# First layer of chunks 3 to 9 as seven block products in place of eight, in a fused attention and feed-forward kernel

## The chip, the cores and the metric

One Trainium2 chip, one core of it. The metric is device time of one launch in microseconds (us), the median of several runs. A core has TensorE (PE, matmuls into PSUM; its weight loads are the row PEld), VectorE (DVE), ScalarE (ACT), GpSimd (POOL) and SyncE (SP), whose queue issues nearly all DMAs here. PSUM has 8 banks, each 128 partitions by 512 f32.

## What is computed

The reference, cut to what matters (8 batches, 8 heads, 576 positions, head size 64, model width 512, hidden width 2048):

```python
k_p = k.reshape(B, H, Sp, 8, D).mean(axis=3)        # 576 keys pooled to 72; v likewise
attn = softmax(q @ k_p.T / sqrt(D)) @ v_p
x = attn.transpose(0, 2, 1, 3).reshape(B, S, 512)
xn = (x - mean(x)) / sqrt(var(x) + 1e-6) * g_ln
out = x + relu(xn @ w_ch1) @ w_ch2                  # 512 -> 2048 -> 512
```

The 4608 rows of x are 36 tiles of 128 tokens, or 9 chunks of 512 tokens (4 tiles each). The code counts chunks from 0, so "chunks 3 to 9" are c = 2 to 8.

## The kernel before, in words

**Arithmetic.** TensorE works in f16 here. Every f32 operand of the two layers is held as a pair of f16 parts, high and low, and a product is three matmuls: high by high, high by low, low by high. The weights come as 8-byte floats; `load_raw` fetches a block of 1 MB, `convert` makes f32 of it, `split_w` scales it and splits it into the pair in `wt`.

**Attention, per tile t.** `stage_a(t)` loads q two tiles ahead, `scores(t)` makes the scores (8 PE instructions, L284), DVE takes the maximum and subtracts it (L293, L294), `probs(t)` runs exp on ACT (L303), casts to f16 (L304), forms the low part on POOL (L311) and transposes the pair by a DMA on SP's queue (L321). `values(t)` multiplies by V (16 instructions, L340 and L341, into PSUM tile `ps_x`; more where a tile lies in two batches), divides by the sums (DVE L354, ACT L361), computes mean and variance and an inverse root (DVE L365 to L383), normalises to `z` (L387), casts to the high part (ACT L391), forms the low part (POOL L392), and transposes the pair into `zT` of its chunk by a DMA (L396).

**Feed-forward, per chunk c.** `ffn_in(c, f)` makes one block of 128 hidden units for all 512 tokens: 4 blocks of the model width times 3 products, 12 matmuls of 512 columns (L415) into one bank of `ps_f`. ACT writes the relu's high part into a ring buffer (L423), DVE its low part (L424). A ring buffer holds a quarter, 4 such blocks. `ffn_out(c, tt, half)` takes the 8 blocks of one half of the hidden width for one tile of tokens: 24 matmuls of 512 columns (L444), and DVE adds the result to x (L454). The second half's result goes out by DMA (L458).

**The order of the work.** Chunks 0 and 1, with the loading, converting and splitting of the weights, follow a list of tokens, `START`: R, C, M and S are the weights' steps, A and B the two attention stages of a tile, HK and HV the pooling of a batch's K and V on POOL, I a quarter of `ffn_in`, O a half of `ffn_out`. From chunk 2 on a loop runs, per chunk, 24 units: 8 `ffn_in`, 4 `ffn_out`, 8 `ffn_in`, 4 `ffn_out`. Before unit number `A_AT[i]` comes the first attention stage of tile i of the next chunk, before `B_AT[i]` the second. A scheduler then orders the instructions of each engine, so that a piece can move some way from where the code has it; each engine works through its order strictly in turn.

**Buffers.** PSUM: 2 banks for scores (`ps_s`), 2 for values (`ps_x`), 4 for the layers (`ps_f`). SBUF: 4 ring buffers, 3 buffers `vr` for loads of V, 2 of `zT`, and 2 buffers of raw weights.

Of the kernel before, what the change touches and what calls it, by code (L numbers as in the profile page):

```python
# [61 lines left out]
def attn_ffn_kernel(ctx: ExitStack, tc: tile.TileContext, qT, kT, v, g, w1, w2, out):  # L62
# [260 lines left out]
    def values(t):  # L323
# [67 lines left out]
        nc.scalar.copy(out=zhl[:, 0, :], in_=z)  # L391
        nc.gpsimd.tensor_tensor(out=zhl[:, 1, :], in0=z, in1=zhl[:, 0, :], op=ALU.subtract)  # L392
# [3 lines left out]
        nc.sync.dma_start_transpose(  # L396
            out=zTs[c][:, :, tt * P : (tt + 1) * P], in_=zhl.rearrange("p a d -> p (a d)")
        )
# [34 lines left out]

# [141 lines left out]
```

## Time and profile before

| | |
|---|---|
| time, median of 3 runs | 895.31 us (894.42 to 897.43) |
| the profiled execution: time, span | 897.94 us, 896.2 us |
| mean granted PE clock | 0.995 of full |
| PE busy | 826.6 us, 92% of the span |
| DVE, ACT, POOL busy | 421.4, 278.8, 259.6 us |
| matmuls of the first layer (L415) | 1824, of them 192 with 256 columns, the rest with 512 |
| matmuls of the second layer (L444) | 1728, all with 512 columns |

The profile is of one execution, whose own time stands beside its span; the 1.7 us between them are outside the instructions. Matmuls overlap in the pipeline, so the time of one alone (some 380 ns for 512 columns) is not what it costs in a row; that is read from the starts of a group.

### The profile page before, as it was taken

What the parts mean: (1) busy time and instruction counts of PE and PEld (TensorE: products, weight loads), DVE (VectorE), ACT (ScalarE), POOL (GpSimd) and SP (SyncE); (2) the same over time, 40 slices, a digit from 0 to 9 for tenths busy, and PEclk for the clock granted to TensorE, in tenths of its full rate; (3) what the DMA queues carried; (4) which work ended last, traced back from release to release, by engine and by line L of the source; (5) the groups of instructions that cost most, each with busy time, mean ns of one, the idle gap of its engine ahead of it and who ended that gap; (6) DMA issues with size and microseconds to landing.
All of it is one profiled execution on the core that took longest, in us unless ns stands there. A gap on an engine that the chain in (4) does not pass through costs nothing.

```text
span 896.2 us, 11921 instructions
## 1 busy us (share of the span) xinstructions
PE 826.6 (92%) x4524; PEld 417.1 (47%) x4524; DVE 421.4 (47%) x970; ACT 278.8 (31%) x529; POOL 259.6 (29%) x414
## 2 busy tenths in 40 slices
PE   2236997999999999999999999999999999999998
PEld 1225744444444444544454545444544454444443
DVE  6587884425643543364335433543354335432121
ACT  2887873313212221233123312331233123311020
POOL 5587783207241340165003610220021002100000
PEclk9999998999999999999999999999999999999999
DMA  8989993102451241254123432341223121310001
GB/s 301 296 219 288 278 269 71 27 4 94 107 128 37 65 101 37 59 145 109 44 53 86 118 65 60 86 89 44 54 59 80 41 54 37 70 47 12 1 1 47
DMA packets 137289, 84.81 MB, mean 95 GB/s; under 512 B 116112, under 2 KB 117264, under 8 KB 135184
## 3 DMA queue, kind: packets, MB, share of 16 engines
q1 hardware_dynamic: 135696, 82.86, 35.2%
q10 hardware_dynamic: 1536, 1.20, 0.5%
q8 instruction: 35, 0.57, 0.3%
q14 instruction: 22, 0.18, 0.1%
HBM read 45.09 MB, written 9.44 MB: 61 GB/s over the span
## 4 chain that ended last, share of the span: by engine, by line
PE 82%; DMA 8%; POOL 6%; issue 2%; ACT 1%; DVE 1%; SPq 1%; POOLq 0%
PE ps_f L444 39%; PE ps_f L415 38%; PE ps_s L284 3%; DMA vr<-in_v_dram 3%; DMA ring<-in_w_dram 1%; POOL vr L234 1%; DMA raw<-in_w_dram 1%; DMA zT<-hl 1%; PE ps_x L340 1%; PE ps_x L341 1%; POOL kr L220 1%; DMA kr<-in_kT_dram 1%; DMA raw<-in_v_dram 1%; POOL kblk L224 1%; POOL kr L221 1%
## 5 line engine op out<-in xcount | busy, mean ns | idle before, releaser
L415 PE MATMUL ps_f<-zT,w 128*128 128x512 f16 (+1 forms) x1824 | 386.3, 371 | 4.4 <-DMA zT<-hl 3.4
L444 PE MATMUL ps_f<-w,ring 128*128 128x512 f16 x1728 | 379.6, 379 | 2.2 <-DVE ring L424 1.2
L415 PEld LDWEIGHTS <-w 128*128 128x128 f16 x1824 | 178.3, 99 | 194.4 <-DMA zT<-hl 3.7
L444 PEld LDWEIGHTS <-ring 128*128 128x128 f16 x1728 | 167.9, 98 | 202.5 <-issue 3.7
L423 ACT ACTIVATE ring<-ps_f 128x512 f16<-128x512 f32 (+1 forms) x152 | 86.6, 573 | 271.0 <-PE ps_f L415 252.4
L424 DVE SCALAR_TENSOR_TENSOR ring<-ps_f,ring 128x512 f16<-128x512 f32 (+1 forms) x152 | 99.7, 660 | 140.5 <-ACT ring L423 138.7
L454 DVE SCALAR_TENSOR_TENSOR x<-ps_f,c_out,x 128x512 f32<-128x512 f32 x72 | 53.8, 749 | 186.8 <-PE ps_f L444 186.8
L311 POOL TENSOR_TENSOR phl<-e,phl 128x512 f16<-128x512 f32 x36 | 42.8, 1190 | 263.9 <-ACT phl L304 262.8
L284 PE MATMUL ps_s<-kblk,q 128*128 128x144 f32 (+1 forms) x320 | 54.6, 333 | 52.8 <-issue 21.8
L392 POOL TENSOR_TENSOR hl<-z,hl 128x512 f16<-128x512 f32 x36 | 42.5, 1181 | 122.4 <-ACT hl L391 120.5
L284 PEld LDWEIGHTS ps_s<-kblk,q 128*128 128x128 f32 (+1 forms) x320 | 47.0, 211 | 60.8 <-issue 39.0
L303 ACT ACTIVATE e<-e 128x576 f32<-128x576 f32 x36 | 24.5, 682 | 155.4 <-DVE e L294 150.8
L361 ACT ACTIVATE x<-ps_x,rs 128x64 f32<-128x64 f32 x144 | 33.3, 312 | 73.5 <-DVE x L354 33.6
L234 POOL TENSOR_TENSOR vr<-vr 72x256 f32<-72x256 f32 x56 | 44.8, 805 | 29.7 <-DMA vr<-in_v_dram 29.2
L224 POOL TENSOR_TENSOR kblk<-kr 64x72 f32<-64x72 f32 x58 | 22.0, 379 | 76.2 <-PE ps_s L284 73.5
L391 ACT CAST hl<-z 128x512 f16<-128x512 f32 x36 | 22.2, 617 | 57.6 <-DVE z L387 57.5
L304 ACT CAST phl<-e 128x1024 f16<-128x1024 f32 x36 | 37.5, 1042 | 6.1 <-issue 3.1
L365 DVE BATCH_NORM_STATS2 st<-x 128x6 f32<-128x512 f32 x36 | 24.9, 692 | 23.4 <-ACT x L361 23.2
L340 PE MATMUL ps_x<-va,pt 128*128 128x65 f16 (+1 forms) x320 | 27.5, 200 | 5.9 <-ACT x L361 4.0
L293 DVE TENSOR_REDUCE mx<-ps_s 128x8 f32<-128x576 f32 x36 | 26.8, 745 | 12.4 <-PE ps_s L284 12.2
L387 DVE TENSOR_SCALAR z<-x,mv,y 128x512 f32<-128x512 f32 x36 | 30.4, 845 | 3.3 <-POOL hl L392 0.8
L380 DVE TENSOR_SCALAR a<-y,ve 128x1 f32<-128x1 f32 x108 | 29.3, 271 | 3.0
(80 smaller groups left out, 470.8 us busy)
## 6 DMA issues: line engine op xcount, KB each, us to landing
raw<-in_w_dram SPq DMA_DIRECT2D x12, 1024.0 KB
q<-in_qT_dram SPq DMA_DIRECT2D x36, 256.0 KB
out_dram<-x SPq DMA_DIRECT2D x36, 256.0 KB
kr<-in_kT_dram SPq DMA_DIRECT2D x30, 288.0 KB
vr<-in_v_dram SPq DMA_DIRECT2D x56, 144.0 KB
ring<-in_w_dram SPq DMA_DIRECT2D x4, 1024.0 KB
raw<-in_v_dram SPq DMA_DIRECT2D x8, 144.0 KB
va<-vh ACTq DMA_DIRECT2D x16, 65.0 KB
```

The costliest lines, as they stand in the source:

```text
L234: eng.tensor_add(out=vr[:, 0:4, :], in0=vr[:, 0:4, :], in1=vr[:, 4:8, :])
L284: nc.tensor.matmul(ps[r, p // 2, p % 2 * 2 * KV : (p % 2 + 1) * 2 * KV], lhsT=q[:, p, r], rhs=kblk[b % NKB][:, p, :], start=True, stop=True,)
L304: nc.scalar.copy(out=ph[:, :, :, 0:KA], in_=e[:, :, 0:KA].unsqueeze(1).broadcast_to([P, 2, H, KA]))
L311: nc.gpsimd.tensor_tensor(out=ph[:, 0, :, KA:P], in0=e[:, :, 0:KA], in1=ph[:, 0, :, 0:KA], op=ALU.subtract)
L340: nc.tensor.matmul(o, lhsT=pt[:, h, r], rhs=VA[b][:, h, :], start=True, stop=False)
L361: nc.scalar.activation(out=xh[:, 4 + i, :], in_=px[:, 1, i, 0:D], func=AF.Copy, scale=rs[:, 4 + i : 5 + i])
L392: nc.gpsimd.tensor_tensor(out=zhl[:, 1, :], in0=z, in1=zhl[:, 0, :], op=ALU.subtract)
L415: nc.tensor.matmul(ps, lhsT=w[:, part, fs], rhs=zT[:, kz, cols], start=(n == 0), stop=(n == 3 * NKT - 1),)
L423: nc.scalar.activation(out=h[:, 0, i, cols], in_=ps, func=AF.Relu)
L424: nc.vector.scalar_tensor_tensor(out=h[:, 1, i, cols], in0=ps, scalar=0.0, in1=h[:, 0, i, cols], op0=ALU.max, op1=ALU.subtract,)
L444: nc.tensor.matmul(ps, lhsT=h[:, part, i, cols], rhs=w[:, wp, j], start=(n == 0), stop=(n == 3 * NFT // 2 - 1),)
L454: nc.vector.scalar_tensor_tensor(out=x, in0=ps, scalar=c_out[:, half : half + 1], in1=x, op0=ALU.mult, op1=ALU.add)
```

## The change

From chunk 2 on, the product of the first layer is done on a 2 by 2 split: the 512 tokens in two halves, the 512 model columns in two halves, the 1024 hidden units of a half of the width in two halves of 512. In place of eight block products there are seven, between sums of blocks (a form of Strassen's method; the table `FACTOR` names the two factors of each). Each product is 2 blocks of the model width times 3, that is 6 matmuls with 256 columns (one half of the tokens).

- **Weights.** `sums_w` forms three sums T2, T3, T4 of the blocks of w1, `sum_last` the fourth, T1, in the place of a block that chunks 0 and 1 no longer need. These are the tokens T and U in `START`, four each.
- **Tokens.** For a tile of the first two of a chunk nothing changes but the place of the transposed pair. For a tile of the last two, `values` normalises the tile two before it once more (`za`), forms the four sums S1 to S4 on DVE, and casts, subtracts and transposes ten blocks (S3, A22, S1, S2, S4) in two pieces of 640 columns in place of one of 512. They go into `zB`, of which there is one; so the transposes of the third tile are held in `pending` and issued at unit 12, behind the last product of the chunk in work.
- **Products.** `ffn_seven(c, h, f)` replaces `ffn_in` for a pair of hidden blocks. Three PSUM banks serve a pair: one takes products 1, 6 and 7 one on top of the other, one 5 and 3, one 2 and then 4. In between ACT copies the partial results to SBUF (four copies of 256 columns per pair), DVE adds to them (four of 256 columns), and relu and low part then run from SBUF (two each of 512 columns).
- **Loop.** 16 units per chunk: 4 `ffn_seven`, 4 `ffn_out`, and again; `A_AT` and `B_AT` are (0, 5, 7, 10) and (4, 6, 11, 12). `ffn_out` takes the two hidden blocks of a pair one after the other, in the order in which the pairs come.
- **Buffers.** 2 ring buffers in place of 4, 2 `vr` in place of 3. Behind `START`, scores and values share one PSUM tile of 2 banks and the layers have 6 banks.
- **START.** O.0.1 goes ahead of I.1.2; R.1.0 and R.1.1 load into the new buffers `tsp`; T and U are put in.

```diff
-A_AT, B_AT = (0, 6, 10, 14), (5, 9, 13, 19)
+A_AT, B_AT = (0, 5, 7, 10), (4, 6, 11, 12)
+FACTOR = {1: ("A11", "B11"), 2: ("A12", "B21"), 3: ("S4", "B22"), 4: ("A22", "T4"), 5: ("S1", "T1"),
+          6: ("S2", "T2"), 7: ("S3", "T3")}
...
-A.10 B.9 I.0.3 S.2.5 S.2.6 HK.3.0 HK.3.1 I.1.2 B.10 S.2.7 O.0.1 I.1.3 A.11 HV.3.0 B.11 HV.3.1 O.1.1
+S.2.5 I.0.3 S.2.6 S.2.7 O.0.1 B.8 T.0.0 HK.3.0 A.10 B.9 T.0.1 HK.3.1 I.1.2 T.1.0 U.0.0 U.0.1 T.1.1 I.1.3
+U.1.0 U.1.1 A.11 HV.3.0 B.10 HV.3.1 B.11 O.1.1
...
-    ring = ctx.enter_context(tc.tile_pool(name="ring", bufs=4))
+    ring = ctx.enter_context(tc.tile_pool(name="ring", bufs=2))
...
+    def split_t(src, dst):
+        nc.scalar.copy(out=dst[:, 0], in_=src)
+        nc.gpsimd.tensor_tensor(out=dst[:, 1], in0=src, in1=dst[:, 0], op=ALU.subtract)
+    def sums_w(h, k):
...
+        for n in range(4):
+            src = block(h, k, *divmod(n, 2))
+            nc.vector.tensor_tensor(out=bs[:, n], in0=src[:, 0], in1=src[:, 1], op=ALU.add)
+        nc.gpsimd.tensor_tensor(out=t1, in0=b12, in1=b11, op=ALU.subtract)
+        nc.vector.tensor_tensor(out=b12, in0=b22, in1=b12, op=ALU.subtract)
+        nc.gpsimd.tensor_tensor(out=b22, in0=b22, in1=t1, op=ALU.subtract)
+        nc.vector.tensor_tensor(out=b21, in0=b21, in1=b22, op=ALU.subtract)
+        for name, src in (("T3", b12), ("T2", b22), ("T4", b21)):
+            T[h, k, name] = spare.pop(0).rearrange("p (a c) -> p a c", a=2)
+            split_t(src, T[h, k, name])
...
-        vraw[b, h] = vr = wk3.tile([KV, POOL, D], F32, name="vr") if vr is None else vr
+        vraw[b, h] = vr = wk2.tile([KV, POOL, D], F32, name="vr") if vr is None else vr
...
+            s3, a22, s1, s2, s4 = (zr[:, i * HC : (i + 1) * HC] for i in range(5))
+            nc.vector.tensor_tensor(out=s1, in0=s3, in1=a22, op=ALU.add)
+            nc.vector.tensor_tensor(out=s2, in0=s1, in1=za[:, :HC], op=ALU.subtract)
+            nc.vector.tensor_tensor(out=s4, in0=za[:, HC:], in1=s2, op=ALU.subtract)
+            nc.vector.tensor_tensor(out=s3, in0=za[:, :HC], in1=s3, op=ALU.subtract)
+            for i in range(2):
+                parts_t(zr, 5 * i, 5, zB[:, i * 10 : i * 10 + 10, (tt - 2) * P : (tt - 1) * P])
...
+    def product(c, h, f, m, start, stop):
...
+        for k in range(KH):
+            w, (zh, zl) = factor(h, k, rname), left(c, lname, k)
+            for part, z in ((0, zh), (0, zl), (1, zh)):
+                nc.tensor.matmul(
+                    ps,
+                    lhsT=w[:, part, f * P : (f + 1) * P],
+                    rhs=z,
...
+    def first_products(c, h, f):
...
+        nc.scalar.copy(out=cc[:, 0, :HC], in_=product(c, h, f, 1, True, False))
+        nc.scalar.copy(out=cc[:, 1, HC:], in_=product(c, h, f, 5, True, False))
+        m2 = product(c, h, f, 2, True, True)
+        nc.vector.tensor_tensor(out=cc[:, 0, :HC], in0=m2, in1=cc[:, 0, :HC], op=ALU.add)
+    def middle_products(c, h, f):
+        cc = C7[f]
+        nc.scalar.copy(out=cc[:, 1, :HC], in_=product(c, h, f, 6, False, False))
+        m3 = product(c, h, f, 3, False, True)
+        nc.vector.tensor_tensor(out=cc[:, 1, :HC], in0=m3, in1=cc[:, 1, :HC], op=ALU.add)
+        nc.scalar.copy(out=cc[:, 0, HC:], in_=product(c, h, f, 4, True, True))
+    def last_product(c, h, f):
+        cc = C7.pop(f)
+        u3 = product(c, h, f, 7, False, True)
+        for j in range(2):
+            nc.vector.tensor_tensor(out=cc[:, j, HC:], in0=u3, in1=cc[:, j, HC:], op=ALU.add)
+        for j in range(2):
...
+            nc.scalar.activation(out=hh[:, 0, f], in_=cc[:, j], func=AF.Relu)
+            nc.vector.scalar_tensor_tensor(
+                out=hh[:, 1, f], in0=cc[:, j], scalar=0.0, in1=hh[:, 0, f], op0=ALU.max, op1=ALU.subtract
+            )
+    def ffn_seven(c, h, f):
+        if f == 0:
+            first_products(c, h, 0)
+        middle_products(c, h, f)
+        if f + 1 < FPQ:
+            first_products(c, h, f + 1)
+        last_product(c, h, f)
```

In the changed kernel the lines of the seven products are: L547 the matmuls, L565, L566, L572 and L575 ACT's copies, L568, L574 and L581 DVE's adds, L587 relu, L588 the low part; L466 is `za`, L470 to L473 the sums S, L484 and L485 the two parts of a piece, L490 its transpose; L612, L622 and L626 are the second layer's matmuls, its addition to x and the store.

**SP's queue where chunk 6 hands over to chunk 7, before** (the attention of chunk 7's last two tiles: `pt` is a transpose of probabilities, `zT` of a normalised tile, `out_dram` the stores of chunk 6, one per `ffn_out` of the second half):

```order
L275 DMA q_6532<-in_qT_dram 128x512
L321 DMA_TRANSPOSE pt_6264<-phl1_105 128x16x128
L396 DMA_TRANSPOSE zT_5930<-hl_6225 128x8x128
L396 DMA_TRANSPOSE zT_5930<-hl_6405 128x8x128
L458 DMA out_dram<-x_5075 128x512
L458 DMA out_dram<-x_5213 128x512
L458 DMA out_dram<-x_5373 128x512
L458 DMA out_dram<-x_5619 128x512
```

The same place now (`zts` holds `zB`):

```order
L332 DMA q_7776<-in_qT_dram 128x512
L378 DMA_TRANSPOSE pt_7445<-phl1_108 128x16x128
L490 DMA_TRANSPOSE zts_92<-hl_7552 128x10x128
L490 DMA_TRANSPOSE zts_92<-hl_7555 128x10x128
L626 DMA out_dram<-x_6010 128x512
L626 DMA out_dram<-x_6128 128x512
L626 DMA out_dram<-x_6461 128x512
L490 DMA_TRANSPOSE zts_92<-hl_7660 128x10x128
L490 DMA_TRANSPOSE zts_92<-hl_7663 128x10x128
L626 DMA out_dram<-x_6639 128x512
```

The last tile's transposes, one before and two now, stood ahead of the four stores and now stand behind three of them; the third tile's two are held until the chunk in work has read `zB` for the last time.

**DVE in the second pass through the first layer of chunk 6, where the scores of chunk 7's last tile fall, before** (`mx` and `e` are the two steps of the scores, `st`, `ve`, `y` steps of an inverse root, `ring` a low part of the hidden units):

```order
L365 BN_STATS st_6208<-x_6183 128x6
L424 SCALAR_TENSOR_TENSOR ring_6165<-ps_f_6229,ring_6165 128x512
L366 BN_AGGR mv2_6209<-st_6208 128x2
L293 TENSOR_REDUCE mx_6247<-ps_s_6248 128x8
L368 TENSOR_SCALAR ve_6212<-mv2_6209 128x1
L294 TENSOR_TENSOR e_6246<-ps_s_6248,mx_6247 128x576
```

The same place now (`raw_2002` holds the partial results of two pairs of hidden blocks):

```order
L581 TENSOR_TENSOR raw_2002<-ps_f_7330,raw_2002 128x256 x2
L350 TENSOR_REDUCE mx_7428<-ps_a_7429 128x8
L588 SCALAR_TENSOR_TENSOR ring_7362<-raw_2002,ring_7362 128x512
L351 TENSOR_TENSOR e_7427<-ps_a_7429,mx_7428 128x576
L588 SCALAR_TENSOR_TENSOR ring_7365<-raw_2002,ring_7365 128x512
L574 TENSOR_TENSOR raw_2002<-ps_f_7397,raw_2002 128x256
L568 TENSOR_TENSOR raw_2002<-ps_f_7484,raw_2002 128x256
L581 TENSOR_TENSOR raw_2002<-ps_f_7389,raw_2002 128x256 x2
L401 TENSOR_SCALAR sm_7504<-ps_a_7507,cv_5553 128x8
```

Between the steps of the scores there was one instruction of the first layer for every 512 columns of hidden units; now there are three for every 512 (two adds, L568 or L574 and L581, and a low part).

More of the change, by code (lines that the diff above doesn't have):

```diff
@@ L72, in attn_ffn_kernel @@
     small = ctx.enter_context(tc.tile_pool(name="small", bufs=3))
-    ps_s = ctx.enter_context(tc.tile_pool(name="ps_s", bufs=1, space=PSUM))
-    ps_x = ctx.enter_context(tc.tile_pool(name="ps_x", bufs=1, space=PSUM))
-    ps_f = ctx.enter_context(tc.tile_pool(name="ps_f", bufs=4, space=PSUM))
+    psum = {}
+    first = ctx.enter_context(ExitStack())
+    for name, bufs in (("ps_s", 1), ("ps_x", 1), ("ps_f", 4)):
+        psum[name] = first.enter_context(tc.tile_pool(name=name, bufs=bufs, space=PSUM))
     wt = {m: const.tile([P, WB + 1, 2, WC], F16, name=f"w{m}") for m in (1, 2)}
+    tsp = [const.tile([P, 2, FPQ, CH], F16, name=f"tsp{i}") for i in range(2)]
+    zts = const.tile([P, 18, CH], F16, name="zts")
     g_sb = const.tile([P, NKT], F32, name="g_sb")
@@ L151, in load_raw @@
     def load_raw(mat, b):
-        raw = ring_tile() if mat == 1 and b < NKT else raw_tile()
+        raw = early_tile() if mat == 1 and b < NKT else raw_tile()
         raws[mat, b] = raw = raw.rearrange("p a f c -> p (a f c)").bitcast(I32)
@@ L385, in values @@
             )
-        Z[t] = z = wk1.tile([P, DM], F32, name="z")
+        c, tt = divmod(t, TPC)
+        seven = c >= 2
+        if seven and tt >= 2:
+            if "z" not in t_raw:
+                t_raw["z"] = t_raw.pop("b").rearrange("p n c -> p (n c)")
+            z = t_raw["z"][:, :DM]
+        else:
+            z = wk1.tile([P, DM], F32, name="z")
+        Z[t] = mv, y
         nc.vector.tensor_scalar(
@@ L407, in ffn_in @@
         h, zT = hT[c, q], zTs[c]
-        ps = ps_f.tile([P, CH], F32, name="ps_f")[:, 0 : cols.stop - cols.start]
+        ps = psum["ps_f"].tile([P, CH], F32, name="ps_f")[:, 0 : cols.stop - cols.start]
         half, j = divmod(f, NFT // 2)
@@ L431, in ffn_in @@
         )
+    PS, C7 = {}, {}
+    def product(c, h, f, m, start, stop):
+        if start and m != 4:
+            PS[f, m] = psum["ps_f"].tile([P, CH], F32, name="ps_f")
+        ps = PS[f, {6: 1, 7: 1, 3: 5, 4: 2}.get(m, m)][:, :HC]
+        lname, rname = FACTOR[m]
+        n = 0
+        for k in range(KH):
[5 more added lines that the diff above has]
+                    rhs=z,
+                    start=start and n == 0,
+                    stop=stop and n == 3 * KH - 1,
+                    skip_group_check=True,
+                )
+                n += 1
+        return ps
@@ L530, in attn_ffn_kernel @@
         ops[name](*map(int, args))
+    first.close()
+    for name, bufs in (("ps_a", 1), ("ps_g", 6)):
+        psum[name] = ctx.enter_context(tc.tile_pool(name=name, bufs=bufs, space=PSUM))
+    psum["ps_s"] = psum["ps_x"] = psum["ps_a"]
+    psum["ps_f"] = psum["ps_g"]
     for c in range(2, NRUN):
```

102 lines of the change are left out of this document (83 added, 19 removed).

## The prediction

> **What bounds the kernel now.** The page first: busy time of the engines, and the span in 40 slices of 22.4 us.
>
> ```profile
> PE 826.6 (92%) x4524; PEld 417.1 (47%) x4524; DVE 421.4 (47%) x970; ACT 278.8 (31%) x529; POOL 259.6 (29%) x414
> PE   2236997999999999999999999999999999999998
> PEclk9999998999999999999999999999999999999999
> ```
>
> From the eighth slice (157 us) on PE is busy without a break, at full clock; the other engines are at half or less. Next the chain of work that ended last, for one pass of the loop (chunk 7, c = 7) and for the last chunk, which has no attention beside it: start, length, work.
>
> ```profile
> 720.16 0.98 PE ps_s L284 x8
> 721.14 12.95 PE ps_f L415 x60
> 734.61 2.59 PE ps_f L415 x12
> 737.20 0.98 PE ps_s L284 x8
> 788.32 20.72 PE ps_f L444 x96
> 809.04 20.72 PE ps_f L415 x96
> 829.76 20.72 PE ps_f L444 x96
> ```
>
> The chain is PE, piece behind piece: the scores of a tile (0.98 us) and, in the gap from 734.09 to 734.61, the values of one (0.52 us); the rest is matmul. A matmul of 512 columns costs 20.72 / 96 = 215.8 ns in a row. From 720.16 to 809.04 are 88.9 us: 4 x 20.72 = 82.9 for the chunk and 6.0 for four tiles' scores and values. So nothing waits there, and PE work taken out of a pass shortens it one for one, until something else is late.
>
> **The products: what goes.** Per chunk 192 matmuls of 512 columns become 2 halves x 4 pairs x 7 products x 6 = 336 of 256. Chunks 0 and 1 have such matmuls already: in START a quarter of chunk 0 is done for half the tokens at a time (the timeline of PE, and the group of that line there with shortest, middle and longest duration):
>
> ```profile
> 96.23 2.78 PE L415 MATMUL ps_f<-zT,w 128*128 128x256 f16 x24
> L415 PE MATMUL ps_f<-zT,w x288: 269/273/634, 80.8 to 165.7; 128*128 128x256 f16 x96, 128*128 128x512 f16 x48
> ```
>
> 24 of them took 2.78 us; less the last one's own 0.27, 23 starts lie 109.1 ns apart. (2.78 / 24 = 115.8 ns counts the pipeline's tail as cost; that is the upper end.) So a chunk's first layer goes from 192 x 215.8 = 41.4 us to 336 x 109.1 = 36.7: 4.77 us less, **33.4 us** for the seven chunks (17.6 at the upper end). I take 33.4: these 24 have a weight load each, as the new ones have. The Trainium skill speaks against that, "TensorE: Matmul & The Clock Gate", Back-to-back issue gap: it says that in a stream of load and matmul pairs a matmul of 128 columns costs some 81 ns where alone it is 56, that is, a short matmul does not hide its load. By it, as an estimate, 25 ns would come on each of 7 x 336 matmuls, 59 us. The row above shows no such cost at 256 columns.
>
> **What comes on the path: the two passes through the first layer.** Per pair ACT gets four copies of 256 columns and two relus of 512, DVE four adds of 256 from PSUM and two low parts of 512. Rows (the groups by form, the first two of the same pass as the windows below, the others of the whole run; the time is the mean in ns ahead of the bar's idle time):
>
> ```profile
> L424 DVE SCALAR_TENSOR_TENSOR ring<-ps_f,ring 128x512 f16<-128x512 f32 x16 | 11.0, 690 | 15.0 <-ACT ring L423 14.7
> L354 DVE TENSOR_TENSOR x<-ps_x,rs 128x256 f32<-128x256 f32 x4 | 1.7, 424 | 0.1
> L423 ACT ACTIVATE ring<-ps_f 128x256 f16<-128x256 f32 x16 | 5.6, 377 | 1.9 <-PE ps_f L415 1.9
> L220 DVE TENSOR_TENSOR kr<-kr 128x288 f32<-128x288 f32 x1 | 0.5, 459 | 1.6 <-DMA kr<-in_kT_dram 1.6
> L234 DVE TENSOR_TENSOR raw<-raw 72x256 f32<-72x256 f32 x4 | 2.4, 601 | 1.0 <-DMA raw<-in_v_dram 1.0
> ```
>
> An add is between 424 ns (L354, PSUM and SBUF in) and 601 (L234, both from SBUF, while POOL does the same work); I take 424, the row with the same operands. The low part I take as L424. A pair is then 4 x 0.424 + 2 x 0.690 = 3.1 us of DVE and 4 x 0.377 + 2 x 0.6 = 2.7 of ACT, in 42 x 0.109 = 4.6 us of PE: alone, that is hidden. With attention it is near the edge (windows: the second pass through the first layer before, then the second pass through the second layer; columns: from and to, length, then busy us of PE, PEld, DVE, ACT, POOL):
>
> ```profile
> 678.70:699.40 20.70, 20.70 (x140) 10.16 (x137) 11.89 (x27) 8.11 (x19) 2.76 (x3) 1.00 0.25 52
> 699.40:720.20 20.80, 20.80 (x99) 9.56 (x97) 5.57 (x15) 1.22 (x2) 1.15 (x1) 1.00 0.16 51
> L293 DVE TENSOR_REDUCE mx<-ps_s 128x8 f32<-128x576 f32 x4 | 3.0, 741 | 0.2 <-PE ps_s L284 0.2
> L294 DVE TENSOR_TENSOR e<-ps_s,mx 128x576 f32<-128x576 f32 x4 | 3.0, 758 | 0.2
> ```
>
> Of DVE's 11.89 us, 8 x 0.69 = 5.5 are low parts, 6.4 attention. Now four pairs take 12.3, the same attention 6.4, and by the order the scores of a second tile fall in (1.5): 20.2 us, for 168 x 0.109 + 2 x 0.98 + 0.52 = 20.8 of PE. DVE is full there; what backs up drains in the second layer, where it has 15 us free. What is behind it: the adds free the PSUM banks. A bank is wanted again 18 matmuls (1.96 us) after its product ended, where before the four banks gave three units of 2.59 us. ACT's casts of probabilities stand in the same queues. I put 1 us of PE waits on each of six such passes (bounds: 0, and 3 with the adds at 601: 16 x 0.18 = 2.8 more of DVE, of which 0.6 fit in, and the round trips): **6 us**. The first pass of a chunk has 12.3 and one tile's scores, and fits.
>
> **The hand-over from chunk to chunk.** Before, the last tile of the next chunk went like this (timeline; its values ended at 696.9), and the DMA of its transpose stopped between 708 and 709 (windows: last two columns the DMA's busy share and GB/s). The last row is the time that such a transpose holds SP's queue, shortest, middle and longest:
>
> ```profile
> 696.97 0.22 DVE L344 TENSOR_SCALAR sm<-ps_x,cvm 128x8 f32<-128x8 f32 x1
> 702.83 0.55 DVE L387 TENSOR_SCALAR z<-x,mv,y 128x512 f32<-128x512 f32 x1
> 703.41 0.62 ACT L391 CAST hl<-z 128x512 f16<-128x512 f32 x1 [3.33 <-DVE z L387]
> 704.11 1.15 POOL L392 TENSOR_TENSOR hl<-z,hl 128x512 f16<-128x512 f32 x1 [14.46 <-ACT hl L391]
> 708.00:709.00 1.00, 1.00 (x7) 0.41 (x6) 0.00 (x0) 0.00 (x0) 0.00 (x0) 1.00 0.41 156
> 709.00:710.00 1.00, 1.00 (x6) 0.48 (x5) 0.16 (x1) 0.00 (x0) 0.00 (x0) 1.00 0.00 0
> L396 SPq DMA_TRANSPOSE zT<-hl x36: 1232/1618/3516, 62.6 to 794.4; - x36
> ```
>
> That is 12 us from values to landing, and 11 us to spare before 720.2. Now the chain is longer: `za` (0.55), four sums of 256 (0.41 each by L220's 1.6 ns a column, 1.6), a cast and a subtraction of 640 columns in place of 512 (0.2 + 0.3), the second piece's subtraction (1.4) and a second transpose on SP's queue (1.62 x 10/8 blocks = 2.0): 6 us more, 18. And it starts later: the order puts these values behind 21 matmuls of the second layer, so 75 x 0.216 + 0.98 for scores + 0.65 for product 1 = 17.8 us are left until product 5 wants `zB`. On SP's queue the two transposes stand behind the store of the third tile, which PE ends 72 x 0.216 + 0.65 + 0.52 = 16.7 us after the first matmul of the 96 that take 20.7: that alone takes all but 5 us of the cover. It is used up; I take 1 us of wait for each of six hand-overs (bounds 0 and 4): **6 us**. The held transposes of the third tile cost nothing: they are due long before.
>
> **START.** T and U put 24 subtractions of 512 on POOL, 24 sums on DVE and 16 casts on ACT. Rows (POOL's groups for a low part and for the three steps that pool V; the windows over PE's unbroken stretch up to the loop, and over its last tokens; on PE's timeline the last token, O.1.1, and the loop's start):
>
> ```profile
> L392 POOL TENSOR_TENSOR hl<-z,hl 128x512 f16<-128x512 f32 x36 | 42.5, 1181 | 122.4 <-ACT hl L391 120.5
> L234 POOL TENSOR_TENSOR vr<-vr 72x256 f32<-72x256 f32 x56 | 44.8, 805 | 29.7 <-DMA vr<-in_v_dram 29.2
> L235 POOL TENSOR_TENSOR vr<-vr 72x128 f32<-72x128 f32 x56 | 25.9, 468 | 0.7
> L236 POOL TENSOR_TENSOR vp<-vr 72x64 f32<-72x64 f32 x56 | 21.2, 392 | 14.6 <-DVE vb L141 14.3
> 166.00:274.00 108.00, 108.00 (x550) 49.72 (x548) 53.20 (x123) 27.97 (x50) 42.97 (x70) 1.00 0.31 80
> 252.00:274.00 22.00, 22.00 (x119) 10.23 (x116) 8.99 (x27) 2.74 (x7) 12.54 (x25) 1.00 0.51 138
> 253.28 20.88 PE L444 MATMUL ps_f<-w,ring 128*128 128x512 f16 x96
> 274.00 13.11 PE L415 MATMUL ps_f<-zT,w 128*128 128x512 f16 x60
> ```
>
> 24 x 1.18 = 28 us fit into POOL's 65 idle us before 274, 24 x 0.82 (L220's rate) = 20 into DVE's 55. At the end it is tight: U.1 waits for I.1.3 on PE (253), and behind it in POOL's queue stand seven V loads to be pooled (7 x 1.67) and the four pieces for `zB`: 2.4 + 11.7 + 4 x 1.45 = 20 of 22 us, with POOL waiting for V's DMA (29.2 us in the run) on two buffers in place of three. The last piece is then done at some 275 and lands 3.7 us later (as from 705.3 to 709 above), where product 5 wants it at 275.3: 3 us. The first 140 us, whose path runs over weights and V, get 1 more for the two buffers. **4 us** (bounds -4 and 14; below nothing, because the scheduler orders all of START anew).
>
> **The sum**, against the profiled execution: 897.9 - 33.4 + 6 + 6 + 4 = 880.5. That execution is 2.6 above the median of the runs; so 877.9 on the median's scale, **878**.
>
> **The rivals.**
>
> The time of each is on the median's scale.
>
> *All of it is covered* (0.22). The scheduler's order already puts other products into the gaps; then 895.3 - 33.4 = 862, with START's 3 us 865. For it: PE did not wait in the passes before. Against: the two sums above without any slack.
>
> *One cover fails* (0.10): 3 us in place of 1 at one of the two places, and 8 in START: 895.3 - 33.4 + 18 + 6 + 8 = 894. For it: neither DVE in the second pass nor the chain at the hand-over has slack. Against: what is late in one pass is not added up, since the second layer's 20.7 us let DVE catch up.
>
> *Slower: the bank's round trip shows in every pair* (0.06). Products 6, 3, 4 and 7 each wait for ACT or DVE to have read what the same bank held. From the end of product 1 to product 6 are 1.96 us. Two relus (1.2) and two copies (0.75) that stand ahead on ACT come to 1.95, and the answer of the semaphores is not in it. It decides from 33.4 / 56 pairs = 0.6 us per pair on; at 0.8 the kernel is at 895.3 + 56 x 0.2 = 906. For it: every pair has the chain. Against: the six banks hold two pairs, and ACT works 2.7 of a pair's 4.6 us.
>
> *Slower: weight loads show* (0.02). The loads take 99 ns each and hide:
>
> ```profile
> L415 PEld LDWEIGHTS <-w 128*128 128x128 f16 x1824 | 178.3, 99 | 194.4 <-DMA zT<-hl 3.7
> ```
>
> A matmul of 109 ns leaves 10. It decides from 33.4 us / 2352 = 14 ns of each load on; with a quarter of it on the path the kernel is at 895.3 - 33.4 + 2352 x 0.025 = 921. The 24 matmuls above speak against it. (The rule on load and matmul pairs quoted from the Trainium skill would have it so.)
>
> For the adds at 601 ns the skill has a rule as well, the Trainium skill's "SBUF — State Buffer", Who interferes with whom: DVE contends with GpSimd where both its inputs lie in SBUF. By it the adds, which read PSUM, stay at the lower price, and the low parts, now both from SBUF, may not; no run here shows those yet.
>
> **How the numbers follow.** My forecast has 0.60. Faster by over 0.3% (about what a measurement of this kernel can tell from no change; below 892.6): 0.60 + 0.22 + 0.04 of the third case = 0.86. Within it: 0.05, of the third. Slower: 0.06 + 0.02 and 0.01 of the third, 0.09. The range goes from 864 (nothing on the path but START) to 894 (one cover gone); it leaves out some 0.1 on each side.
>
> **What would show it.** Right: L547's matmuls some 109 ns apart in the last chunk, whose first layer takes 2 x 18.3 us; a pass of about 86 us in place of 88.9, with PE's waits in its second pass (released by ACT or DVE) and at the first product 5 of a chunk (released by DMA `zts`), each near 1 us; the loop's start at about 278 in place of 274. Wrong: waits above 3 us at a hand-over, a wait in every pair, or a start of the loop later than 288; and, on the other side, passes of 84 us, in which nothing waits.

## The result and the profile after

The changed kernel takes 902.95 us (median of 14 runs, 897.27 to 905.22), the kernel before 897.1 (14 runs, 894.42 to 902.34): a ratio of 1.0056, 95% interval 1.0036 to 1.0077. Forecast were 878 and a range from 864 to 894: the kernel is 0.6% slower, clear of noise, where faster was forecast. The profiled execution took 904.0 us, its span is 902.2.

The page of the changed kernel (engines, then slices of 22.6 us):

```profile
PE 801.6 (89%) x5532; PEld 516.5 (57%) x5532; DVE 556.6 (62%) x1288; ACT 368.7 (41%) x783; POOL 324.4 (36%) x452
PE   2234994999889899999989998999999999999998
PEclk9999997899999899999999999999999999999999
POOL 5487676033755525313540156114201130121000
```

PE's busy time has gone down by 25 us, from 826.6, but its unbroken stretch now begins only behind the 25th slice (564 us; before, at 157). Up to there slices of only 8 tenths stand in it, and its clock falls to 7 and 8 tenths in slices 7, 8 and 14. POOL's row has up to 8 in that part, and at most 4 behind the 25th slice. Chunk by chunk (counted from 0; START ends with chunk 1), from DVE's timeline (the end of a chunk's eighth addition of a result, L454 before, L622 after):

| | chunk 1 ends | 2 | 3 | 4 | 5 | 6 | 7 | 8 |
|---|---|---|---|---|---|---|---|---|
| before: us of each | 274.9 | 88.0 | 88.9 | 90.4 | 88.9 | 89.8 | 88.9 | 82.9 |
| after | 297.6 | 90.9 | 88.0 | 91.1 | 83.9 | 85.5 | 84.1 | 78.1 |

So START costs 22.7 us, chunks 2 to 5 gain 2.3 together, chunks 6 to 8 gain 13.9; with 0.5 gained behind the last addition that is the 6.0 by which the spans differ. (These are single executions; START's length differs by some us between executions: 279.5 and 275.1 to the end of chunk 1 in two whose START is the same, nosums_noprep and hold below.) Chunks 6 to 8 do what the sum of the products says (4.3 to 4.8 each). The last chunk's chain, for the second half (start, length, work):

```profile
859.44 16.38 PE ps_f L547 x150
875.82 1.51 PE ps_f L612 x7
877.33 1.31 PE ps_f L547 x12
878.64 0.86 PE ps_f L612 x4
880.16 18.36 PE ps_f L612 x85
```

150 matmuls of 256 columns in 16.38 us: 109.2 ns each. PE waits for nothing in this chunk, neither for a bank nor for a weight load.

Two passes of the changed kernel (windows; columns as in the prediction), chunk 4's and chunk 7's, and two of before, chunk 3's and chunk 6's:

```profile
476.74:567.03 90.29, 86.98 (x651) 58.36 (x650) 57.27 (x140) 35.36 (x83) 33.87 (x50) 0.98 0.40 94
737.24:820.38 83.14, 83.14 (x618) 56.73 (x617) 52.56 (x129) 33.96 (x82) 14.58 (x14) 1.00 0.29 63
```
```profile
363.18:452.10 88.92, 88.92 (x482) 43.91 (x481) 40.05 (x98) 23.48 (x49) 29.35 (x52) 1.00 0.34 88
631.36:721.14 89.78, 89.78 (x506) 44.05 (x504) 39.02 (x88) 22.87 (x48) 10.81 (x12) 1.00 0.25 59
```

The late pass has 14 operations on POOL, the early one 50: K and V of later sequences are pooled in the passes of chunks 2 to 5 (and, as shown below, already at the end of START). Before, PE covered both kinds of pass. The prediction read its slack from the quiet kind alone (its windows, 678.7 to 720.2, lie in chunk 6).

Where PE waited, first in START and then in chunk 3's pass (the waits: for what, us in total, times, longest):

```profile
PE ps_f L516 <- DMA zts<-hl: 9.4, 1, 9.4
PE ps_f L547 <- DVE x L622: 5.0, 1, 5.0
...
PE ps_a L397 <- DMA pt<-phl: 3.5, 2, 2.9
```

How the first came about, on DVE (timeline, rows between left out). `raw<-w` is a sum of T, `w<-w,raw` and `w<-w,ws` convert weights, the `z` rows are chunk 1's tiles:

```profile
127.92 2.48 DVE L250 TENSOR_TENSOR raw<-w 128x512 f32<-128x512 f16 x4
131.72 3.86 DVE L189 SCALAR_TENSOR_TENSOR w<-w,raw 128x1024 int32<-128x1024 int32 x1 [0.23 <-ACT raw L186]
136.35 3.50 DVE L154 SCALAR_TENSOR_TENSOR w<-w,ws 128x1024 f16<-128x1024 f32 x1
142.35 1.41 DVE L252 TENSOR_TENSOR raw<-raw 128x512 f32<-128x512 f32 x1
144.49 2.48 DVE L452 TENSOR_SCALAR z<-x,mv,y 128x512 f32<-128x512 f32 x1
152.30 0.53 DVE L452 TENSOR_SCALAR z<-x,mv,y 128x512 f32<-128x512 f32 x1
```

Sums that nobody needs before the loop stand ahead of the `z` that PE needs next (152.3; its transpose landed at 157.5). And the same operation `z` takes 0.53 us once and 2.48 at another time; single sums (L250) took from 0.67 to 3.96 us. POOL was at work from 130 to 149 with one pause of 1.0 us.

The second wait, at the loop's start: the addition that frees PE's bank stood in DVE's queue behind the maximum of a V, and that one waited 4.92 us for POOL to pool this V:

```profile
295.90 0.68 DVE L297 TENSOR_REDUCE mv<-vp 72x1 f32<-72x512 f32 x1 [4.92 <-POOL vp L293]
296.88 0.74 DVE L622 SCALAR_TENSOR_TENSOR x<-ps_f,c_out,x 128x512 f32<-128x512 f32 x1
```

This V is the first that is pooled for the loop; the scheduler moved it to the end of START.

How the `pt` wait came about in chunk 3's pass, DVE's rows, then POOL's, then PE's:

```profile
443.01 0.76 DVE L350 TENSOR_REDUCE mx<-ps_a 128x8 f32<-128x576 f32 x1
443.69 3.37 DVE L588 SCALAR_TENSOR_TENSOR ring<-raw,ring 128x512 f16<-128x512 f32 x2
446.98 0.74 DVE L351 TENSOR_TENSOR e<-ps_a,mx 128x576 f32<-128x576 f32 x1
...
451.43 1.85 POOL L291 TENSOR_TENSOR vr<-vr 72x256 f32<-72x256 f32 x2 [3.67 <-DMA vr<-in_v_dram]
453.24 0.86 POOL L292 TENSOR_TENSOR vr<-vr 72x128 f32<-72x128 f32 x2
454.07 1.16 POOL L368 TENSOR_TENSOR phl<-e,phl 128x512 f16<-128x512 f32 x1
...
460.61 0.20 PE L397 MATMUL ps_a<-va,pt 128*128 128x65 f16 x1 [2.88 <-DMA pt<-phl]
```

Two low parts of the products took 3.37 us in place of 1.4, so `e` was 2 us late; then the probabilities' low part (L368), ready at some 450, stood in POOL's queue behind V's load and pooling: 4 us. From scores to values are 18 us, where the passes before had 13 to 14.

A wait can be paid for twice. The windows around another such wait, in chunk 4's pass, and behind it (third from last: granted clock):

```profile
544.00:548.00 4.00, 1.33 (x20) 0.71 (x19) 1.94 (x7) 0.82 (x2) 0.00 (x0) 1.00 0.77 174
548.00:552.00 4.00, 4.00 (x17) 1.49 (x14) 3.75 (x10) 1.76 (x6) 3.69 (x6) 0.57 0.03 7
```

PE waited 2.67 us, then ran 4 us at a clock of 0.57, which costs 4 x 0.43 = 1.7 us more. The Trainium skill, "TensorE: Matmul & The Clock Gate", Part 1, says that a window of some 3.4 us without work halves the clock until one with work has passed. The depth agrees (0.50 from 298 to 302, behind the 5.0 us at the loop's start). The length does not: here a wait of 2.67 us, shorter than that window, went ahead of the low clock, and another of 2.9 us (at 458) was followed by full clock.

### The profile page after: what moved, and what is told of

Its sections match the earlier page's. It is cut to its first block, busy times and chain, and to the rows that moved or that the text cites. A ratio compares the mean times of both kernels' runs of the same rounds, so it can differ in the third digit from the quotient of the medians.

```text
span 902.2 us, 14789 instructions
## 1 busy us (share of the span) xinstructions
PE 801.6 (89%) x5532; PEld 516.5 (57%) x5532; DVE 556.6 (62%) x1288; ACT 368.7 (41%) x783; POOL 324.4 (36%) x452
## 4 chain that ended last, share of the span: by engine, by line
PE 63%; DMA 12%; POOL 11%; DVE 7%; ACT 3%; issue 2%; SPq 1%; ACTq 0%; POOLq 0%
PE ps_f L612 32%; PE ps_f L547 22%; DMA vr<-in_v_dram 6%; PE ps_f L516 5%; DMA kr<-in_kT_dram 3%; POOL vr L291 3%; PE ps_a L341 2%; DMA pt<-phl 2%; POOL vr L292 1%; DVE raw L250 1%; POOL hl L485 1%; POOL phl L368 1%; POOL kr L277 1%; DVE w L189 1%; POOL vp L293 1%
## 5 line engine op out<-in xcount | busy, mean ns | idle before, releaser
L612 PE MATMUL ps_f<-w,ring 128*128 128x512 f16 x1728 | 386.1, 382 | 4.4 <-DVE w L154 2.8
L612 PEld LDWEIGHTS <-ring 128*128 128x128 f16 x1728 | 168.4, 98 | 200.6 <-issue 10.9
L547 PE MATMUL ps_f<-zts,w 128*128 128x256 f16 x1680 | 207.9, 275 | 5.0 <-DVE x L622 5.0
L547 PEld LDWEIGHTS <-w 128*128 128x128 f16 x1680 | 164.4, 99 | 28.3 <-DVE x L622 5.1
L622 DVE SCALAR_TENSOR_TENSOR x<-ps_f,c_out,x 128x512 f32<-128x512 f32 x72 | 53.7, 746 | 93.6 <-PE ps_f L612 91.4
L341 PE MATMUL ps_a<-kblk,q 128*128 128x144 f32 (+1 forms) x320 | 55.5, 334 | 52.0 <-issue 23.3
L516 PE MATMUL ps_f<-zts,w 128*128 128x512 f16 (+1 forms) x480 | 89.3, 347 | 12.2 <-DMA zts<-hl 9.4
L547 PE MATMUL ps_f<-zts,tsp 128*128 128x256 f16 x672 | 95.4, 273 | 1.1 <-DVE rowmax L119 1.1
L587 ACT ACTIVATE ring<-raw 128x512 f16<-128x512 f32 x112 | 64.9, 625 | 59.1 <-DVE raw L581 55.5
L588 DVE SCALAR_TENSOR_TENSOR ring<-raw,ring 128x512 f16<-128x512 f32 x112 | 82.7, 760 | 7.4 <-ACT ring L587 6.7
L341 PEld LDWEIGHTS ps_a<-kblk,q 128*128 128x128 f32 (+1 forms) x320 | 46.5, 211 | 59.1 <-issue 39.1
L485 POOL TENSOR_TENSOR hl<-z,hl 128x512 f16<-128x512 f32 x22 | 26.3, 1198 | 129.3 <-ACT hl L484 129.1
L547 PEld LDWEIGHTS <-tsp 128*128 128x128 f16 x672 | 65.2, 98 | 10.7 <-issue 1.6
L368 POOL TENSOR_TENSOR phl<-e,phl 128x512 f16<-128x512 f32 x36 | 42.6, 1183 | 77.7 <-ACT phl L361 77.4
L485 POOL TENSOR_TENSOR hl<-raw,hl 128x640 f16<-128x640 f32 x28 | 39.6, 1431 | 69.8 <-ACT hl L484 69.8
L581 DVE TENSOR_TENSOR raw<-ps_f,raw 128x256 f32<-128x256 f32 x112 | 42.2, 418 | 28.9 <-PE ps_f L547 25.6
L565 ACT COPY raw<-ps_f 128x256 f32<-128x256 f32 x56 | 20.9, 374 | 72.5 <-PE ps_f L547 67.0
```

What stands on the lines that cost most here:

```text
L341: nc.tensor.matmul(ps[r, p // 2, p % 2 * 2 * KV : (p % 2 + 1) * 2 * KV], lhsT=q[:, p, r], rhs=kblk[b % NKB][:, p, :], start=True, stop=True,)
L368: nc.gpsimd.tensor_tensor(out=ph[:, 0, :, KA:P], in0=e[:, :, 0:KA], in1=ph[:, 0, :, 0:KA], op=ALU.subtract)
L485: nc.gpsimd.tensor_tensor(out=zhl[:, 1, :], in0=src, in1=zhl[:, 0, :], op=ALU.subtract)
L516: nc.tensor.matmul(ps, lhsT=w[:, part, fs], rhs=zT[:, kz, cols], start=(n == 0), stop=(n == 3 * NKT - 1),)
L547: nc.tensor.matmul(ps, lhsT=w[:, part, f * P : (f + 1) * P], rhs=z, start=start and n == 0, stop=stop and n == 3 * KH - 1, skip_group_chec ...
L581: nc.vector.tensor_tensor(out=cc[:, j, HC:], in0=u3, in1=cc[:, j, HC:], op=ALU.add)
```

## The experiments

Theories: V (the third `vr` buffer), S (the sums of T and U in START), P (K and V's pooling on POOL in the loop), against Q (the seven products themselves fill DVE and ACT); later H (the hold: a DVE operation with all operands in SBUF takes longer while POOL works). Where a chunk's length is given, it is from the one profiled execution.

**The ring alone, in the kernel before** (b_vr2).

```diff
-        vraw[b, h] = vr = wk3.tile([KV, POOL, D], F32, name="vr") if vr is None else vr
+        vraw[b, h] = vr = wk2.tile([KV, POOL, D], F32, name="vr") if vr is None else vr
```

> The kernel before, with two vr buffers in place of three and nothing else. Theory V (the third vr buffer that the change took is what costs; POOL waits for V's loads and all that stands behind it in POOL's queue is late): the loop starts at 285 us or later in place of 274, POOL's waits for vr loads rise from 29 us to some 50, and the time is 905 to 920. Theory S (the sums T and U in START cost): nothing but the ring changes, so the loop starts at 274 to 277 and the time stays within 3 us of the kernel before.

903.42 us, ratio 1.008 (1.0052 to 1.0108). Chunk 1 ends at 279.4, not 285 or later, and the time stays below the 905 that V expected: V holds (S expected no change), though smaller than expected. POOL's waits for V (before, then with two buffers):

```profile
POOL vr L234 <- DMA vr<-in_v_dram: 29.2, 15, 3.9
```
```profile
POOL vr L234 <- DMA vr<-in_v_dram: 53.0, 26, 5.2
```

**The ring back in the changed kernel** (vr3_q2).

```diff
-        vraw[b, h] = vr = wk2.tile([KV, POOL, D], F32, name="vr") if vr is None else vr
+        vraw[b, h] = vr = wk3.tile([KV, POOL, D], F32, name="vr") if vr is None else vr
-        q_sb[t] = wk3.tile([P, NPAIR, P], F32, name="q")
+        q_sb[t] = wk2.tile([P, NPAIR, P], F32, name="q")
```

> The changed kernel with three vr buffers again; the room is taken from q, which gets two buffers in place of three. Theory V: the loop starts at some 277 us in place of 298, the passes of chunks 2 to 4 take 84 to 86 us in place of 88 to 91, without waits for pt, and the time is 865 to 878. Theory S: the loop still starts at 290 or later, passes as in the changed kernel, 897 to 903. If q's ring is short in its place, PE's waits name q's load.

896.5 us, ratio 0.9989 (0.997 to 1.0009): 6.5 less than the changed kernel, the same amount as in the kernel before, and far from V's 865 to 878. Chunk 1 ends at 291.9; chunks 2 to 5 take 92.5, 87.2, 88.2, 87.7, in sum 355.6, where it was 353.9. So V is 6 us of START and none of the loop; none of PE's waits names q's load.

**Without the arithmetic of T and U** (nosums), **and with the ring back** (nosums_vr3).

```diff
-        for n in range(4):
-            src = block(h, k, *divmod(n, 2))
-            nc.vector.tensor_tensor(out=bs[:, n], in0=src[:, 0], in1=src[:, 1], op=ALU.add)
...
+        if name[0] == "T":
+            name = {"T1": "B12", "T2": "B22", "T3": "B11", "T4": "B21"}[name]
```

> The changed kernel without the arithmetic of T and U: the products take plain weight blocks for T1 to T4, so the output is not the reference's; ring of two vr buffers kept. Theory V: the loop still starts at 288 or later and passes 1 to 3 stay at 88 to 91, time 892 to 903. Theory S: the loop starts at 272 to 279 us, passes 1 to 3 as in the changed kernel, time 878 to 884. A third possibility, the new order of START by itself: neither this nor the ring moves the start.

> Both edits: no arithmetic of T and U (output not the reference's) and three vr buffers (q two). Theories V and S together cover all of the loss in START and in passes 1 to 3: loop's start at 274 to 277, every pass at 84 to 86, time 862 to 868. If the new order of START costs by itself, the loop starts at 282 or later here too.

889.06 us, ratio 0.9911 (0.988 to 0.9941), chunk 1 ends at 281.1; with the ring 883.66, 0.9859 (0.983 to 0.9888), 277.3. S is 14 us, nearly all in START; chunks 2 to 5 (90.8, 88.3, 90.6, 83.1 and 92.4, 89.8, 87.5, 88.4) gain next to nothing. START's new order by itself is out as a cause of more than some 3 us (277.3; its sign was 282 or later). Both times are above what S, and V and S together, expected (878 to 884, 862 to 868): from 883.7 to the 863.7 of the products alone, 20 us stay open.

**The adds without the splits** (adds_only).

```diff
-        for name, src in (("T3", b12), ("T2", b22), ("T4", b21)):
-            T[h, k, name] = spare.pop(0).rearrange("p (a c) -> p a c", a=2)
-            split_t(src, T[h, k, name])
...
-        split_t(t_raw["t1"][:, h * KH + k], T[h, k, "T1"])
```

> The changed kernel with the 24 sums of T and U on DVE and the 8 on POOL kept, but without their 16 casts on ACT and 16 subtractions on POOL (the products take plain weight blocks, so the output is not the reference's). If DVE's sums, between the evictions and the conversions in DVE's queue, are what costs in START: chunk 1 ends at 293 to 298 as in the changed kernel, time 898 to 903. If POOL's subtractions cost, ahead of V and hl in POOL's queue: chunk 1 ends at 281 to 285, time 889 to 893.

902.08 us, ratio 1.0069 (1.0052 to 1.0085); chunk 1 ends at 295.4. It is the sums, not their splits on ACT and POOL. Nor is it that the sums were stretched: here the 24 on DVE took 18.9 us in all, none over 1.64 (26.5 in the changed kernel), and yet PE waits 14.0 us for the transpose of the `z` behind them.

**No K and V pooling in the loop** (noprep).

```diff
-                        prep_k(b)
-                        prep_v(b)
+                        VA[b], VB[b], CV[b] = VA[b - 2], VB[b - 2], CV[b - 2]
```

> The changed kernel without the pooling of K and V for later sequences inside the loop (their loads and POOL work left out, old K and V used, so the output is not the reference's). Theory P (in chunks 2 to 5 the sevens' gain is eaten because a tile's chain from scores to pt is longer than its cover where POOL also pools K and V, in order and behind their loads): chunks 2 to 5 take 83 to 86 us each in place of 90.9, 88.0, 91.1 and 83.9, PE's waits for pt vanish, the start of the loop stays at 298, time 885 to 890. Rival Q (the seven products themselves fill DVE and ACT in those chunks): passes of 88 to 91 stay, time 900 to 904.

882.03 us, ratio 0.9834 (0.9815 to 0.9852). Chunks 2 to 5 take 84.8, 84.1, 85.0, 84.1, and PE waits for nothing in them: P stands, Q falls. (The edit also takes out the loads of K and V and the small steps behind the pooling on DVE and ACT; it does not tell these apart.) Chunk 1 ends at 291.9, 5.7 earlier, which P did not expect: without the V that was pooled at START's end, PE's wait of 5.0 us at the loop's start is 0.3.

**The probabilities' low parts on DVE in the loop** (phl_dve).

```diff
-        nc.gpsimd.tensor_tensor(
+        eng = nc.vector if "ps_g" in psum else nc.gpsimd
+        eng.tensor_tensor(
             out=ph[:, 0, :, KA:P], in0=e[:, :, 0:KA], in1=ph[:, 0, :, 0:KA], op=ALU.subtract
...
```

> The changed kernel with the low parts of the probabilities in the loop on DVE in place of POOL, so that a tile's pt does not stand in POOL's queue behind V's loads. If it is POOL's queue (in order) that makes pt late: the waits for pt in chunks 2 to 4 go from 2 to 3 us to under 1, time 893 to 898. If it is DVE that is late (its own queue, or DVE and POOL holding each other up over SBUF), the waits stay or grow, time 902 to 908.

894.75 us, ratio 0.9979 (0.996 to 0.9998). The waits for `pt` shrink to 0.4 us, though one of 2.4 for the maximum of a V comes up; chunks 2 to 5 take 88.2, 88.1, 87.7, 82.6, 7 us less. So the low parts' place on POOL is about half of P's 16. This is not order alone: with less work on POOL, DVE's 64 low parts of the products in these chunks take 45.7 us in all in place of 51.4 (44.9 in noprep).

**Half of the sums moved into chunk 2** (late_vr3, with the ring back; T1 is made in the same step).

```diff
-S.2.5 I.0.3 S.2.6 S.2.7 O.0.1 B.8 T.0.0 HK.3.0 A.10 B.9 T.0.1 HK.3.1 I.1.2 T.1.0 U.0.0 U.0.1 T.1.1 I.1.3
-U.1.0 U.1.1 A.11 HV.3.0 B.10 HV.3.1 B.11 O.1.1
+S.2.5 I.0.3 S.2.6 S.2.7 O.0.1 B.8 T.0.0 HK.3.0 A.10 B.9 T.0.1 HK.3.1 I.1.2 I.1.3
+A.11 HV.3.0 B.10 HV.3.1 B.11 O.1.1
...
+            if c == 2 and u in (1, 2):
+                sums_w(1, (1, 2).index(u))
```

> Three vr buffers (q two) and only the first half's sums in START; the second half's T and U are made in chunk 2's first half, ahead of its units 1 and 2, where DVE and POOL have idle time. If the sums cost in START because of where they stand: chunk 1 ends at 283 to 286 in place of 292 with all sums in START, chunk 2 grows by less than 2 us, time 887 to 891. If they cost as much wherever they stand: chunk 2 grows by 6 to 8 us, time 895 to 897.

895.65 us (892.55 to 897.3), ratio 0.9987 (0.9964 to 1.001). In its profile chunk 1 ends at 285.4 and chunk 2 takes 90.7, as theory S has it; but that is the fastest of four executions, and the median is only 0.9 below vr3_q2's. Inconclusive.

**All three causes gone** (nosums_noprep: nosums, noprep, and the ring back).

> The changed kernel without the arithmetic of T and U, without the pooling of K and V in the loop (output not the reference's), and with three vr buffers (q two). If those are all the causes: chunk 1 ends at 274 to 277, every pass at 84 to 85.5 and the last at 78, time 863 to 868, that is, all of the products' 33 us. If something else in START or in the loop costs: 872 or more.

864.33 us, ratio 0.9641 (0.961 to 0.9673): 32.9 us less than the kernel before, measured alongside (897.21), which is all but 0.5 of the products' 33.4. Chunk 1 ends at 279.5 (its execution, 870.32, is 6.0 above the median), chunks 2 to 8 take 84.8, 84.1, 85.0, 84.1, 85.5, 84.1, 78.1. PE's waits from there on, all of them:

```profile
PE ps_f L536 <- DVE x L611: 0.3, 1, 0.3
```

**Only the sums' place** (pin).

```diff
+    def sums_late(h, k):
+        with tc.issue_after(zop[7].ins):
+            sums_w(h, k)
...
```

> The changed kernel with one thing altered: the sums of T and U are queued on their engine behind the z of chunk 1's last tile, in place of ahead of it. Theory S (the sums cost where they stand in DVE's queue, ahead of that z): PE's wait of 9.4 us at 157 us falls below 4, chunk 0 ends at 192 to 197 in place of 202.4, chunk 1 at 288 to 293 in place of 297.6, time 894 to 899. If the sums cost by their sheer work, wherever they stand: chunk 1 still ends at 296 to 299, time 901 to 904.

893.52 us, ratio 0.9964 (0.9945 to 0.9984), 9.4 less than the changed kernel. Chunk 0 ends at 192.8 in place of 202.4, and chunk 1 at 288.9. The wait only falls to 6.3 us, not below 4, but it is over at 148 in place of 157. The same work, queued behind one `z`, costs 9 us less. The sums themselves took no less (27.9 us of DVE in place of 26.5), the weight conversions in START 43.9 in place of 48.1.

**The hold by itself** (hold: 40 additions on POOL beside chunk 8, in the kernel in which nothing waits).

```diff
...
+                with tc.issue_after(hop[0].ins):
+                    for i in range(40):
+                        nc.gpsimd.tensor_tensor(out=d[:, i % 2], in0=d[:, 2], in1=d[:, 3], op=ALU.add)
```

> The hold by itself: the kernel without the arithmetic of T and U and without K and V's pooling in the loop (output not the reference's), in which PE waited for nothing from chunk 2 on; added are 40 additions of 128x512 f32 on POOL, back to back (some 50 us), beside chunk 8's first layer and second layer, which have no attention. Nothing waits for them. Theory H: DVE's low parts, which read and write SBUF, rise from 0.69 to 2 us or more each while POOL works, the additions from PSUM stay at 0.42, and chunk 8 takes 5 us or more longer. Theory Q (it is only the order in POOL's queue): the low parts stay below 0.8 and chunk 8 at 78 us.

The groups of the kernel without these additions, then POOL's row and DVE's groups with them (while POOL works):

```profile
L577 DVE SCALAR_TENSOR_TENSOR ring<-raw,ring 128x512 f16<-128x512 f32 x8 | 5.3, 690 | 1.2 <-ACT ring L576 1.1
L570 DVE TENSOR_TENSOR raw<-ps_f,raw 128x256 f32<-128x256 f32 x8 | 3.0, 419 | 2.6 <-PE ps_f L536 2.6
```
```profile
779.86 52.66 POOL L708 TENSOR_TENSOR tsp<-tsp 128x512 f32<-128x512 f32 x40
L577 DVE SCALAR_TENSOR_TENSOR ring<-raw,ring 128x512 f16<-128x512 f32 x8 | 11.8, 1514 | 1.1 <-ACT ring L576 1.1
L570 DVE TENSOR_TENSOR raw<-ps_f,raw 128x256 f32<-128x256 f32 x8 | 3.0, 414 | 0.7 <-PE ps_f L536 0.7
```

The low parts, with both inputs in SBUF, rise from 690 to 1514 ns (2 us or more were expected); the additions from PSUM stay where they were. The hold is shown. Its expected price, 5 us or more, is not: chunk 8 took 79.0 us in place of 78.1; DVE had idle time there, 38 us busy of 79 (time 866.55, ratio 0.9664, 0.9641 to 0.9687; 2.2 over the kernel without, which was not measured alongside). A hold costs time only where something that PE will wait for stands behind it in DVE's queue, as at the loop's start in best1 below.

**Together** (best1: ring back, phl_dve, sums pinned, the second half's in chunk 2; best3: the same with two `vr` buffers).

> All that the runs point to, together: three vr buffers (q two); low parts of the probabilities in the loop on DVE; the sums queued behind the z of chunk 1's last tile, those of the second half made in chunk 2. If the three losses are separate and add: chunk 1 ends at 279 to 284, chunks 2 to 5 at 84 to 88 each, time 873 to 880. If they replace one another (the next queue is late instead): chunk 1 ends at 286 or later, time 885 to 890.

> As the combined kernel, but with the change's two vr buffers (and three q). The ring's worth in it: if it is as in the kernel before and in the changed kernel, 5 to 7 us more than the combined kernel; if moved sums have taken away the crowding that made V's loads late, under 2 us more.

best1: 883.44 us, ratio 0.9847 (0.9823 to 0.9872); it beats both kernels, but lies between the 873 to 880 of separate losses and the 885 to 890 of losses that replace one another; chunk 2 took 91.5, not 84 to 88. best3: 890.41, 0.991 (0.9882 to 0.9939); the ring is again worth 7.0. What was late in best1 was the loop's start, where PE waited 6.0 us (DVE's timeline, then POOL's):

```profile
274.68 5.07 DVE L255 TENSOR_TENSOR raw<-w 128x512 f32<-128x512 f16 x2
279.68 0.74 DVE L626 SCALAR_TENSOR_TENSOR x<-ps_f,c_out,x 128x512 f32<-128x512 f32 x1
...
275.60 1.39 POOL L489 TENSOR_TENSOR hl<-raw,hl 128x640 f16<-128x640 f32 x1
276.95 0.45 POOL L295 TENSOR_TENSOR vr<-vr 72x128 f32<-72x128 f32 x1
277.36 1.84 POOL L489 TENSOR_TENSOR hl<-raw,hl 128x640 f16<-128x640 f32 x1
```

Two sums of chunk 2 were held for 5 us, until POOL paused (279.2), and the addition that frees PE's bank stood behind them.

**These two sums out of the way** (best4: the loop's sums behind START's last addition; best5: START's also behind chunk 1's first eviction).

```diff
+                with tc.issue_after(zop["x"].ins):
+                    sums_w(1, (1, 2).index(u))
```

> The combined kernel, with the second half's sums in chunk 2 queued behind START's last addition of a result on DVE. Theory H (a DVE operation with all its operands in SBUF is held while POOL works on SBUF; two sums took 5.07 us at the loop's start, ahead of the addition that frees PE's bank): PE's wait of 6.0 us at the loop's start goes below 1 and its clock stays at 1.00 there, chunk 1 ends at 274 to 276 in place of 280.4, time 875 to 879. If the wait has another cause (the new PSUM pools wait for all of START): it stays at 4 to 6, time 882 to 885.

> As the kernel before it in this call, with the first half's sums queued behind the first eviction of chunk 1 in place of behind the z of its last tile. Theory H: the 4 us that PE still waits at 144 us go below 2, time 1 to 4 us less than that kernel. If that wait is no work of the sums: no difference beyond 1.5 us.

best4: 883.8 us, ratio 0.9853 (0.983 to 0.9875), not the 875 to 879 expected: the wait at the loop's start falls from 6.0 to 1.4 us, but product 5 then waits 3.8 us for `zB`. best5: 881.77, 0.9822 (0.9784 to 0.9861), the lowest of the full kernels, though not clear of best1. In best5 the wait at the loop's start is down to 0.7 us. So its cause was the sums ahead of the addition, and not the rival, the new PSUM pools; that the hold, and not only the place, made it 6 us is read from the 5.07 us above. The time hardly falls, because another wait takes its place a few microseconds on:

```profile
PE ps_f L552 <- DMA zts<-hl: 4.5, 1, 4.5
PE ps_f L552 <- DVE x L627: 0.7, 1, 0.7
```

That is product 5 waiting for `zB`. The wait at 144 us in best1 (4.1) is still 4.4 at 148 in best5, where below 2 was expected: what holds it is open. Of the 33 us of the products, best5 keeps 15.5.

## Why the prediction was wrong

Two steps failed: START's term, and the terms for the passes of the loop. The products' term held. Two of the signs of being wrong that the prediction names came, one on each side: the loop starts later than 288 (297.6), and chunks 6 and 7 are passes in which nothing waits (85.5 and 84.1 us).

- **The products, −33.4**: right. 109.2 ns each in the last chunk, −4.8 us per chunk there, and −32.9 in the kernel from which the other causes were taken.
- **The second pass through the first layer, +6, and the hand-over, +6**: wrong as placed. In nosums_noprep PE waits 0.3 us from chunk 2 on, and in chunks 6 to 8 of the changed kernel for nothing. A DVE that on paper adds up to 20 us in 20.8 did not delay PE, nor did a chain with no slack on paper: the prediction put a price on a full sum without a row that waits.
- **What the loop lost instead, 16.8 us in chunks 2 to 5** (2.3 gained in place of 19.1): not in the prediction. It failed in taking one quiet pass (10.8 us of POOL) for all six that carry attention. In chunks 2 to 5 of before POOL worked 16 to 29 us: there V's loads and pooling stand in front of the probabilities, and POOL's work stretches DVE's low parts, which the change had moved from PSUM to SBUF. noprep gives back 15.9 of it, phl_dve 7.3.
- **START, +4 (bounds −4 and 14)**: it cost 22.7. The step "24 x 0.82 = 20 into DVE's 55" counted idle time over 108 us, put the sums at nothing for it, and did not ask where in the queue they would stand. The size was near (18.9 us in adds_only, 26.5 in the changed kernel); the place was not asked for. Without the sums chunk 1 ends 16.5 us earlier; with their place alone altered (pin) 8.7. "1 more for the two buffers" was 4.5 (b_vr2) to 5.7 us (vr3_q2) of START. These parts overlap and do not add up.
- **START's last step** (product 5 waits 3 us for `zB` at the loop's start): not seen in the changed kernel, whose loop starts after the wait of 5.0 us behind the maximum of V, a wait that the prediction did not have. Where that one is short, such a wait appears: 4.5 us in vr3_q2 and best5, 3.8 in best4.
- **The rivals**: the bank's round trip and the loads did not show. The round trip's 906 lies nearest to the measured time, but by chance, since in chunks 6 to 8 no pair waits; "one cover fails" (894) named two places that did not fail. The rule on shared SBUF ports was quoted there for the low parts and then not priced, for them or for the sums. It would have spoken against the change: the Trainium skill, "SBUF — State Buffer", Who interferes with whom, says that DVE operations with two SBUF inputs, and some copies and `tensor_scalar` forms, contend with GpSimd, and that one then blocks the other. The runs agree (1514 against 690 ns). Additions with one input from PSUM and one from SBUF stay untouched (414 against 419 ns), as it says of operations with at most one SBUF input.

Not settled: how much of S and P is order and how much is hold. pin and phl_dve give 9 and 8 us, but both alter the hold along with the order: in pin the weight conversions take 4.2 us less, in phl_dve the low parts 5.7. For S, adds_only speaks for order: sums that are hardly stretched cost as much. hold shows the other at work, but not its share.

## What to carry to other kernels

Read slack from the busiest pass of a loop, not from a typical one: this change was hidden in passes with 11 us of POOL and laid bare in those with 16 to 29. Extra work "in idle time" needs a place as well as a length: ask what stands behind it in its engine's queue, and what runs on POOL while DVE reads SBUF. And take one wait away only with an eye on the next: the 6.0 us at the loop's start became 4.5 at product 5.
